# A new order of loads and steps in the first stage of a fused forgetting-attention and MLP kernel

## The chip, the cores and the metric

The kernel runs on one core of a Trainium2 chip. The metric is the device time of one execution in microseconds (us), the median over the runs of one comparison; lower is better. Profiles are of one execution each, with the engines TensorE (PE; PEld is its weight loads), VectorE (DVE), ScalarE (ACT), GpSimd (POOL) and SyncE (SP).

## The reference

Attention with a forget gate over 8 batches, 8 heads, 576 positions and 64 values per head, followed by an MLP over the 4608 tokens (512 to 2048 to 512) with a tanh GELU:

```python
scores = scale * np.matmul(q, k.transpose(0, 1, 3, 2))
cum = np.cumsum(np.log(np.clip(f, 0.0001, 1.0)), axis=-1)
scores = np.where(causal, -1e9, scores + cum[:, :, :, None] - cum[:, :, None, :])
attn = softmax(scores)                       # over keys
x = np.matmul(attn, v)                       # then (b, s) x (h, d): 4608 x 512
h = x @ w_in                                 # 512 x 2048
out = gelu_tanh(h) @ w_out                   # 2048 x 512
```

Inputs and output are float32.

## The kernel before

**Units of work.** The 64 pairs of batch and head are taken as 16 quads of four heads. Quad `i` belongs to batch `i // 2`. The MLP goes over 9 chunks of 512 tokens. For a quad, queries and keys are loaded as bf16 (`q_c`, `k_c`, two buffers each, by the parity of the quad), turned on VectorE (`qT`, `kT`), multiplied on TensorE in three score rounds (`ps_s`), put through the exponential on ScalarE into `pt`, masked on the diagonal, and multiplied with the values. The gate enters as a weight on each key: `vw` is v times this weight, and `w_bf` holds the weights that give the denominators.

**An order written out by hand.** There is no scheduler: the string `FRONT` (and `SECOND`, `STEADY`, `FLUSH`, `LAST` for later chunks) is a list of words, and `run` (L807) executes them one by one, which appends their instructions to the engines' queues. Every engine works through its own queue in that order and waits where an operand is not there yet or a buffer is still being read. What stands between two words on another engine's queue does not matter to an engine; what stands ahead on its own queue does. A word `X@Y` makes the load X wait also for Y (`after`, L176). The words that matter here, with the number of the quad or chunk as first argument:

- `LK.i`, `LQ.i`: load k or q of quad i, issued on GpSimd's queue (L208, 288 KB each). `LC.1.t`: tile t of v of batch 1, on GpSimd's queue too (L185, 256 KB; tile 4 is half). `LV.b.h`: half of v of batch b, on SP's queue, behind the stores of the output. `WI.n`, `WO.n`: pieces of w_in, and quarters of w_out (L201, 512 KB as bf16), on GpSimd's queue.
- `TK.i`, `TQ.i`: transposes of k and q on VectorE (L214).
- `S.i.r`: score round r of quad i on TensorE (L277) with its two exponentials on ScalarE (L285); `H.i.r.g` is half of one. Two buffers of PSUM serve the rounds.
- `M`: mask by a select on GpSimd (L291). `m`: mask by a product with a triangle on VectorE (L321).
- `VW.i`: `vw` of quad i on GpSimd (L231), `vw.i`: the same on VectorE. `CL.i`: copies 64 rows of `vw` on VectorE (L236).
- `D.i`: denominators: 24 matmuls (L347), then on VectorE den, rec and rb (L366 to L370). `V.i.x`, `v.i.x`: half of the attention output (L347), which VectorE multiplies by rb into `xT` (L379). The second group of matmuls of `V` reads the rows that `CL` copied. D and V share one PSUM buffer.
- `J`, `I.c.p`: first MLP product with GELU. `F.c.n`: the next n steps of the second MLP product of chunk c. For chunk 0 a step is one of 64 (four output tiles of 128 tokens, 16 steps of 128 hidden features each; L667). Quarter c of w_out serves steps 4c to 4c + 3 of each tile. When a tile is done, VectorE copies it (L672) and SP stores it; two PSUM buffers take turns. `F` uses a step as one matmul of the whole array, `f` as four matmuls of 32 columns.
- `U.k`, `UW.u.k`, `G`: sums of weight blocks and of GELU blocks on VectorE that save multiplications in later chunks. `X`: loads ScalarE's table for the exponential.

The loads on GpSimd's queue:

```python
def load_w_out(c):
    n = N_FT // 4
    return nc.gpsimd.dma_start(out=w_out_sb[:, n * c:n * (c + 1), :],
                        in_=w_out_hbm[:, n * c:n * (c + 1), :])
```

The functions that the words name, and the loop that reads them:

```python
def load_values(b, half):
    return load_v(b, 4 * half, 4)
...
"F": out_part,
"f": lambda c, n: out_part(c, n, 1),
```

Of the kernel before, what the change touches and what calls it, by code (L numbers as in the profile page):

```python
# [16 lines left out]
def kernel(  # L17
# [12 lines left out]
    B, H, S, D = q.shape  # L30
# [44 lines left out]
    FRONT = """  # L75
        Z TQ.0 LP.2 TR WI.1 TQ.1 S.0.0 B.1.384 CW WI.0 TK.1 S.0.2 LP.4 LP.3 B.1.512 vw.0.0 B.2.512 H.1.0.1 H.1.1.1 WI.3 M.0.0 W vw.1.0 WI.2 B.2.512
        WI.5 H.1.0.0 D.0.0 M.1.0.1 M.1.0.0 H.0.1.1 V.0.0.0 H.0.1.0 M.0.1 LQ.2 V.0.1.0 B.1.256 H.1.1.0 D.1.0 WI.4 H.0.3.0 WI.6 B.1.256 V.1.0.0 H.0.3.1
        WI.7 LK.2 V.1.1.0 m.0.3.2 H.1.3.0 j.0.0 vw.0.1 H.1.3.1 LC.1.4 m.0.3.4 D.0.1 M.1.3 S.1.2 M.1.1 VW.1.1 V.0.0.1 WO.0 V.0.1.1 LC.1.2 D.1.1
        WO.2@m.0.3.4 J.0.1 J.0.2 WO.1 LC.1.0@VW.1.1 WO.3@m.0.3.2 V.1.0.1 V.1.1.1 LC.1.1 GJ.0.0 LC.1.3 TK.2 J.1.1 LK.3 J.0.3 J.1.0 LQ.3 TQ.2 LQ.4 VW.3
        J.1.3 LK.4 J.1.2 F.0.4 X F.0.4 S.2.0 F.0.11 TK.3 S.2.2 F.0.6 LV.2.0 TQ.3 F.0.4 LK.5 S.2.1 F.0.2 F.0.7 TQ.4 m.2.1 S.3.0 vw.2 CL.2 M.2.2 f.0.7  # L80
        M.2.0 D.2 S.3.1 f.0.7 LQ.5 V.2.0 m.3.0 S.3.2 TK.4 LK.6@LQ.4 f.0.1 f.0.3 V.2.1 M.3.2 f.0.2 S.4.1 CL.3 m.3.1 LQ.6 f.0.5 TQ.5 H.4.2.1 D.3 H.4.0.1
        H.4.0.0 VW.4 V.3.1 v.3.0 f.0.1 H.4.2.0 U.0 m.4.1 LV.2.1@m.3.1 I.1.1 LQ.7@CL.3 I.1.4 TQ.6 I.1.6 m.4.2.3 I.1.0 m.4.2.2 I.1.5 CL.4 U.3 LV.3.0@LQ.7
        U.1 TK.6 I.1.2 M.4.0 U.2 G.0 TK.5 UW.2.1 I.1.3 I.1.7 G.1.1.2 F.1.16 X UW.2.2 S.5.0 UW.2.3 LQ.8 F.1.19 S.5.1 D.4 VW.5 M.5.0 f.1.13 S.5.2 V.4.0
        f.1.14 V.4.1 UW.2.4 m.5.2.3 m.5.2.2 CL.5 M.5.1 S.6.0 f.1.13 D.5 S.6.1 f.1.4 LK.7 V.5.1 f.1.3 f.1.10 vw.6 S.6.2 m.6.1 M.6.2.2 m.6.0 V.5.0
        LV.3.1@LK.6 f.1.5 CL.6 LK.8 m.6.2.3
    """

    SECOND = """
# [32 lines left out]
    def many(n, shape, dtype, name):  # L121
        return [singles.tile(shape, dtype, name=f"{name}{i}") for i in range(n)]
# [11 lines left out]
    vw = many(2, [128, NT + 1, 4, D], BF16, "vw")  # L134
# [724 lines left out]
```

## Time and profile before

| | before |
|---|---|
| time, median of 3 runs | 324.79 us (324.18 to 325.45) |
| profiled execution, its own time | 326.56 us |
| its span on the core | 324.3 us |
| TensorE busy | 310.0 us (96%) |
| VectorE busy | 241.7 us (75%) |
| ScalarE busy | 212.6 us (66%) |
| GpSimd busy | 107.0 us (33%) |
| granted TensorE clock | 1.0 of full speed |
| read from HBM, written | 36.85 MB, 9.44 MB |

A row of a timeline begins with its start and its duration in us from the start of the span, then the engine, the line of the kernel, the operation, what it writes and reads with shapes, how many instructions were merged, and in brackets the idle time of the engine ahead of it with what ended it. A row of waits gives the total, the number and the longest. A row of DMA issues gives the size and the time from issue to landing. The page's busy times are of the whole span. A matmul's end is modelled, so a wait on TensorE is better read from the starts of neighbouring rows.

### The profile page before, as it was taken

Reading aid. Unit: us, or ns where it says so; the run is one execution under the profiler, and the core shown is the slowest. Engines: PE = TensorE matmul, PEld = TensorE weight load, DVE = VectorE, ACT = ScalarE, POOL = GpSimd, SP = SyncE. Lnnn points to the kernel's source line nnn. Section 1 sums busy time; section 2 is a strip of 40 time slices with the busy share of each in tenths; the row PEclk is TensorE's granted clock in tenths of the full one; section 3 lists DMA queues with packets and bytes.
Section 4 is the critical chain, followed back from the end, with each engine's and each line's share of the span. In section 5 each row is a group of like instructions: output and inputs, shape, how many; then the busy total and the mean of one; then the engine's idle time right before and its main releaser. Section 6 shows DMA issues by size and latency. Waiting matters only on the chain.

```text
span 324.3 us, 11816 instructions
## 1 busy us (share of the span) xinstructions
PE 310.0 (96%) x5337; PEld 221.2 (68%) x5337; DVE 241.7 (75%) x374; ACT 212.6 (66%) x242; POOL 107.0 (33%) x145
## 2 busy tenths in 40 slices
PE   0799989999999999999999999999999999999996
PEld 0557844454677667776788877767776786788785
DVE  3664307998989978779876998599885866597574
ACT  4495667686766786678667876877587743846610
POOL 8868507253111405510752056305610150000000
PEclk9999999999999999999999999999999999999999
DMA  6999999577034951395119610981001011010202
GB/s 117 232 155 165 196 250 217 139 160 143 8 67 88 227 116 36 76 213 107 36 40 211 143 40 6 206 183 35 7 32 67 17 35 53 16 50 2 99 33 98
DMA packets 47490, 33.41 MB, mean 103 GB/s; under 512 B 29776, under 2 KB 42192, under 8 KB 47440
## 3 DMA queue, kind: packets, MB, share of 16 engines
q0 software_dynamic: 9632, 15.99, 28.4%
q1 hardware_dynamic: 37664, 16.60, 18.9%
q8 instruction: 41, 0.67, 0.8%
q14 instruction: 9, 0.07, 0.1%
q10 hardware_dynamic: 144, 0.07, 0.1%
HBM read 36.85 MB, written 9.44 MB: 143 GB/s over the span
## 4 chain that ended last, share of the span: by engine, by line
PE 82%; DMA 6%; POOL 4%; ACT 4%; DVE 2%; issue 1%; POOLq 0%; DVEq 0%
PE ps_w L600 30%; PE ps_h L395 19%; PE po L347 9%; PE ps_q L520 8%; PE ps_s L277 8%; DMA w_out_sb<-in_moe_w_out_dram 4%; PE ps_u L468 4%; PE pso L667 4%; DMA q_c<-in_q_dram 2%; ACT pt L285 2%; POOL pt L291 1%; POOL w_out_sb L201 1%; POOL v_nat L185 1%; POOL w_in_sb L197 1%; PE cum_ps L721 1%
## 5 line engine op out<-in xcount | busy, mean ns | idle before, releaser
L285 ACT ACTIVATE pt<-ps_s 128x1024 bf16<-128x1024 f32 (+2 forms) x100 | 93.9, 990 | 41.3 <-PE ps_s L277 37.1
L291 POOL TENSOR_SCALAR_AFFINE_SELECT pt<-pt 128x512 bf16<-128x512 bf16 (+3 forms) x65 | 40.8, 639 | 98.0 <-ACT pt L285 75.2
L395 PE MATMUL ps_h<-xT,w_in_sb 128*128 128x512 bf16 (+1 forms) x320 | 66.8, 358 | 0.3 <-ACT gT L403 0.2
L395 PEld LDWEIGHTS <-w_in_sb 128*128 128x128 bf16 x320 | 31.2, 98 | 26.7 <-issue 0.6
L600 PEld LDWEIGHTS <-gT 128*32 128x32 bf16 (+1 forms) x1216 | 44.2, 97 | 5.5 <-issue 2.2
L403 ACT ACTIVATE gT<-ps_h 128x1024 bf16<-128x1024 f32 x34 | 34.6, 1017 | 18.7 <-PE ps_h L395 18.4
L600 PE MATMUL ps_w<-w_out_sb,gT 128*32 128x256 bf16 (+1 forms) x1008 | 42.6, 273 | 0.0
L277 PE MATMUL ps_s<-qT,kT 32*128 32x64 bf16 (+5 forms) x896 | 36.3, 263 | 4.6 <-DVE qT L214 4.3
L600 PEld LDWEIGHTS <-gsum 128*32 128x32 bf16 (+1 forms) x948 | 35.5, 97 | 3.6 <-issue 1.3
L231 POOL TENSOR_TENSOR vw<-v_nat,wT 128x1280 bf16<-128x1280 f32 (+1 forms) x13 | 29.6, 2278 | 11.8 <-DMA v_nat<-in_v_dram 11.5
L536 DVE TENSOR_TENSOR usnap<-ps_q,usnap 128x1024 f32<-128x1024 f32 x15 | 17.9, 1222 | 18.6 <-PE ps_q L520 13.2
L277 PEld LDWEIGHTS <-kT 32*128 32x128 bf16 x896 | 16.5, 93 | 20.9 <-issue 11.5
L600 PE MATMUL ps_w<-usum,gsum 128*32 128x256 bf16 (+1 forms) x791 | 29.9, 273 | 0.0
L617 DVE COPY snap<-ps_w 128x512 f32<-128x512 f32 x32 | 21.8, 681 | 6.1 <-PE ps_w L600 6.0
L531 ACT ACTIVATE gT<-usnap 128x1024 bf16<-128x1024 f32 x15 | 15.8, 1054 | 12.1 <-DVE usnap L536 11.8
L379 DVE TENSOR_TENSOR xT<-po,rb 128x576 bf16<-128x576 f32 x26 | 19.5, 752 | 5.6 <-PE po L347 5.3
L347 PE MATMUL po<-pt,vw 128*32 128x64 bf16 (+4 forms) x624 | 22.4, 278 | 0.0
L214 DVE STREAM_TRANSPOSE qT<-q_c 128x576 f32<-128x576 f32 x16 | 19.8, 1247 | 2.7 <-DMA q_c<-in_q_dram 2.5
L214 DVE STREAM_TRANSPOSE kT<-k_c 128x576 f32<-128x576 f32 x16 | 19.5, 1248 | 3.1 <-DMA k_c<-in_k_dram 3.1
L347 PEld LDWEIGHTS <-vw 128*32 128x32 bf16 x672 | 14.8, 97 | 9.3 <-issue 2.8
L208 POOL DMA_DIRECT2D k_c<-in_k_dram x16 | 9.1, 569 | 33.7 <-DVE kT L214 17.4
L520 PEld LDWEIGHTS <-w_in_sb 128*128 128x128 bf16 x160 | 15.6, 98 | 2.5 <-issue 0.4
(134 smaller groups left out, 478.4 us busy)
## 6 DMA issues: line engine op xcount, KB each, us to landing
out_dram<-o_st SPq DMA_DIRECT2D x35, 256.0 KB, 2.3
k_c<-in_k_dram POOLq DMA_DIRECT2D x16, 288.0 KB, 5.2
q_c<-in_q_dram POOLq DMA_DIRECT2D x16, 288.0 KB, 6.2
v_nat<-in_v_dram SPq DMA_DIRECT2D x16, 256.0 KB, 5.3
v_nat<-in_v_dram SPq DMA_DIRECT2D x20, 128.0 KB, 4.9
v_nat<-in_v_dram POOLq DMA_DIRECT2D x8, 256.0 KB, 8.2
w_in_sb<-in_moe_w_in_dram POOLq DMA_DIRECT2D x8, 256.0 KB, 7.6
w_out_sb<-in_moe_w_out_dram POOLq DMA_DIRECT2D x4, 512.0 KB, 11.1
```

What stands on the lines that cost most here:

```text
L214: return nc.vector.transpose(out=dst.rearrange("p s c -> p (s c)").bitcast(FP32) .rearrange("p (t a) -> p a t", a=S // 32), in_=src.rearra ...
L231: return eng.tensor_mul(vw[i % 2][:, t0:t1], vb[:, t0:t1, h0:h0 + 4, :], wT[:, i, t0:t1, :].unsqueeze(3).to_broadcast([128, t1 - t0, 4, D]))
L277: nc.tensor.matmul(tiles[h // 2][:, h % 2, c0:c0 + nq], key_columns(i, key, h, c), qq[32 * h:32 * h + 32, q0:q0 + nq, c], start=(c == 0 an ...
L285: nc.scalar.activation(p[:, 2 * g:2 * g + 2, off:off + n], t[:, :, 0:n], AF.Exp, scale=scale)
L291: nc.gpsimd.affine_select(out=x, in_=x, compare_op=ALU.is_ge, fill=0.0, base=0, pattern=pattern, channel_multiplier=-1)
L347: nc.tensor.matmul(po[r0:r0 + w.shape[-1], 448 + q0:448 + q0 + nq], w, p[:, h, col:col + nq], start=(key in (0, "low")), stop=(key in ("lo ...
L379: nc.vector.tensor_mul(xT[:, 2 * u + x, r0 + s0:r0 + s1], po, rbs[i, part])
L395: nc.tensor.matmul(ph[:, j, n * cols:(n + 1) * cols], w_in_sb[:, dt, 128 * ft:128 * ft + 128], xT[:, dt, h0:h0 + cols], start=(dt == 0 and ...
L403: nc.scalar.activation(gelus(c, 2 * pr, 2), ph, AF.Gelu_apprx_tanh)
L520: nc.tensor.matmul(ps[:, k, HC * n:HC * n + HC], w[:, d, 128 * n:128 * n + 128], x[:, d, :], start=(first and n == 0 and d == 0), stop=(d ...
L600: nc.tensor.matmul(ps[c0:c0 + width, n, cols[0]:cols[1]], x[:, j, 128 * n + c0:128 * n + c0 + width], w[:, j, cols[0]:cols[1]], start=(fir ...
L617: copy(kept[name], ps)
```

## The change

Only the string `FRONT` changes, from the word behind `WI.7` on; no operation is added or taken away. What it does:

- The quarters of w_out are issued as 0, 1, 2, 3 one behind the other (before: 0, a v tile, 2, 1, a v tile, 3), then k and q of quad 3, then four tiles of v of batch 1, then `LQ.4` and `LK.4`.
- `VW.3` moves on GpSimd's queue from behind `LQ.4` to behind the masks `M.2.2` and `M.2.0`.
- On VectorE, `TK.3` and `TQ.3` move ahead of the first copy of an output tile, `TQ.4` behind `m.2.1` and `vw.2`, `CL.2` behind the denominators of quad 2.
- The 64 steps of chunk 0 are dealt out anew between the score rounds, most of them as `F`: before 4, 4, 11, 10, 9, 7, 7, 4, 2, 5, 1; after 9, 11, 10, 9, 8, 6, 2, 3, 5, 1.
- Later in the string `U.0`, `m.4.1`, `TK.4`, `VW.4`, `UW.2.1`, `UW.2.2`, `I.1.2`, `I.1.3`, `I.1.7` change places with neighbours, and `LV.3.1` waits for `LQ.7` instead of `LK.6`.

```diff
-        ... V.0.0.1 WO.0 V.0.1.1 LC.1.2 D.1.1
-        WO.2@m.0.3.4 J.0.1 J.0.2 WO.1 LC.1.0@VW.1.1 WO.3@m.0.3.2 V.1.0.1 V.1.1.1 LC.1.1 GJ.0.0 LC.1.3 TK.2 J.1.1 LK.3 J.0.3 J.1.0 LQ.3 TQ.2 LQ.4 VW.3
-        J.1.3 LK.4 J.1.2 F.0.4 X F.0.4 S.2.0 F.0.11 TK.3 S.2.2 F.0.6 LV.2.0 TQ.3 F.0.4 LK.5 S.2.1 F.0.2 F.0.7 TQ.4 m.2.1 S.3.0 vw.2 CL.2 M.2.2 f.0.7
-        M.2.0 D.2 S.3.1 f.0.7 LQ.5 V.2.0 m.3.0 S.3.2 TK.4 LK.6@LQ.4 f.0.1 f.0.3 V.2.1 M.3.2 f.0.2 S.4.1 CL.3 m.3.1 LQ.6 f.0.5 TQ.5 H.4.2.1 D.3 H.4.0.1
-        H.4.0.0 VW.4 V.3.1 v.3.0 f.0.1 H.4.2.0 U.0 m.4.1 LV.2.1@m.3.1 I.1.1 LQ.7@CL.3 I.1.4 TQ.6 I.1.6 m.4.2.3 I.1.0 m.4.2.2 I.1.5 CL.4 U.3 LV.3.0@LQ.7
-        U.1 TK.6 I.1.2 M.4.0 U.2 G.0 TK.5 UW.2.1 I.1.3 I.1.7 G.1.1.2 F.1.16 X UW.2.2 S.5.0 ...
+        ... V.0.0.1 WO.0 V.0.1.1 D.1.1 WO.1@m.0.3.4
+        J.0.1 J.0.2 WO.2 WO.3 LK.3 LQ.3 V.1.0.1 V.1.1.1 LC.1.2 LC.1.0@m.0.3.4 LC.1.3 GJ.0.0 LC.1.1 TK.2 J.1.1 J.0.3 TQ.2 J.1.0 J.1.3 LQ.4 LK.4 J.1.2
+        F.0.4 F.0.5 X TK.3 TQ.3 S.2.0 F.0.11 S.2.2 F.0.10 LV.2.0 LK.5 S.2.1 F.0.9 m.2.1 vw.2 S.3.0 TQ.4 F.0.8 M.2.2 M.2.0 D.2 VW.3 S.3.1 CL.2 F.0.6
+        LQ.5 V.2.0 m.3.0 TK.4 S.3.2 LK.6@LQ.4 f.0.2 M.3.2 V.2.1 F.0.1 f.0.2 S.4.1 CL.3 m.3.1 LQ.6 F.0.5 TQ.5 H.4.2.1 D.3 H.4.0.1 H.4.0.0 V.3.1 v.3.0
+        f.0.1 H.4.2.0 VW.4 m.4.1 U.0 LV.2.1@m.3.1 I.1.1 I.1.4 LQ.7@CL.3 UW.2.1 TQ.6 I.1.6 I.1.0 m.4.2.3 m.4.2.2 I.1.5 CL.4 U.3 LV.3.0@LQ.7 U.1 I.1.2
+        TK.6 M.4.0 U.2 I.1.3 I.1.7 G.0 TK.5 G.1.1.2 X UW.2.2 F.1.16 S.5.0 ...
```

## The prediction

> **What bounds the kernel now.** I read the page first, then TensorE's waits, then the timelines of TensorE, GpSimd and VectorE between 28 and 90 us, and last the DMA issues over short stretches, which give each load's time to landing.
>
> ```profile
> PE 310.0 (96%) x5337; PEld 221.2 (68%) x5337; DVE 241.7 (75%) x374; ACT 212.6 (66%) x242; POOL 107.0 (33%) x145
> ...
> PE 82%; DMA 6%; POOL 4%; ACT 4%; DVE 2%; issue 1%; POOLq 0%; DVEq 0%
> ```
>
> TensorE is busy 310.0 of 324.3 us; the first matmul group after the start-up begins at 9.86, and behind it almost nothing is idle. So a wait removed from TensorE shortens the kernel by its full length, a new one lengthens it by as much, and nothing later absorbs either. The chain's 6% of DMA is where to look. The waits of TensorE between 20 and 120 us have one row:
>
> ```profile
> PE pso L667 <- DMA w_out_sb<-in_moe_w_out_dram: 1.3, 2, 0.7
> ```
>
> ```profile
> 41.95 1.03 PE L667 MATMUL pso<-w_out_sb,gT 128*128 128x512 bf16 x4
> 43.58 1.02 PE L667 MATMUL pso<-w_out_sb,gT 128*128 128x512 bf16 x4 [0.60 <-DMA w_out_sb<-in_moe_w_out_dram]
> 44.53 0.70 PE L277 MATMUL ps_s<-qT,kT 32*128 32x64 bf16 x24
> 45.16 1.04 PE L667 MATMUL pso<-w_out_sb,gT 128*128 128x512 bf16 x4
> 46.86 1.67 PE L667 MATMUL pso<-w_out_sb,gT 128*128 128x512 bf16 x7 [0.66 <-DMA w_out_sb<-in_moe_w_out_dram]
> 48.47 0.63 PE L277 MATMUL ps_s<-qT,kT 32*128 32x320 bf16 x16
> 49.03 2.33 PE L667 MATMUL pso<-w_out_sb,gT 128*128 128x512 bf16 x10
> 51.30 0.64 PE L277 MATMUL ps_s<-qT,kT 32*128 32x64 bf16 x16
> 51.86 2.12 PE L667 MATMUL pso<-w_out_sb,gT 128*128 128x512 bf16 x9
> 53.91 0.74 PE L277 MATMUL ps_s<-qT,kT 32*128 32x64 bf16 x24
> ```
>
> A row's first number is its start. From start to start, ten F steps take 2.27 us and nine take 2.05: 0.22 each and 0.1 for the switch to scores. The four at 41.95 need 0.87 and hold 1.63 (43.58 - 41.95), so the first wait is really 0.76; the four at 45.16 hold 1.70, so the second is 0.83. The busy figure hides the tail of a matmul. Together the waits on w_out are **1.6 us**, all that the new order of loads can return.
>
> **The loads.** All these loads go through GpSimd's queue, and land in the order of issue. Landings before: quarter 0 of w_out 37.2, a v tile 38.0, quarter 2 41.0, quarter 1 43.5, a v tile 44.3, quarter 3 46.8, two v tiles 47.5 and 48.3, LK.3 49.6, LQ.3 51.0, LQ.4 52.5. The differences are prices: a quarter 2.5 to 3.1 us, a v tile 0.75, k or q of a quad 1.4. In the new order: quarter 0 at 37.2, quarters 1 and 2 at 40.3 and 42.8, quarter 3 at 46.8 less the two v tiles (1.5) = 45.3, LK.3 46.7, LQ.3 48.1, four v tiles to 51.1, LQ.4 52.5. The ninth load behind a given one waits for it (LK.3, issued at 37.48, for quarter 0), so the last two v tiles are issued behind the landing of quarters 0 and 1, at 37.4 and 40.4, ten us before their turn: free.
>
> F.4 F.5 now run from 41.95 to 44.0 and need quarter 2 at 43.7: no wait. S.2.0 to 44.6; F.11 asks for quarter 3 at 44.6 + 3 x 0.22 = 45.27: a wait of 0.1 (bounds 0 and, at 3.1 for each quarter, 1.3). Score rounds now follow at S.2.2 47.1, S.2.1 49.9, S.3.0 52.5 (before 48.5, 51.3, 53.9). ScalarE needs some 2.6 us from one round to the next in its buffers (51.30 to 53.91), and every new distance has that, F.9 exactly.
>
> **VectorE's order.** TK.3 and TQ.3 now stand ahead of the copy of output tile 0, so the copy waits for LQ.3: TQ.3 48.1 to 49.35, copy to 50.0. Tile 2 needs that buffer at the third step of F.9, 50.95: hidden by 0.9 us, beyond which each us that LQ.3 is late costs one.
>
> **F for f.** F replaces most f. A run of F that ends in an attention product pays the 0.1 us switch; column-wise f steps do not (28 matmuls, 7 steps, 54.58 to 56.10 = 1.52, nothing over). F.8 before D.2, F.6 before V.2.0 and F.1 between V.2.1 and f.2: 0.2 to 0.4 us; I take 0.35.
>
> **VW.3 moved behind M.2.0.** This decides the sign.
>
> ```profile
> 48.43 2.33 POOL L231 TENSOR_TENSOR vw<-v_nat,wT 128x1280 bf16<-128x1280 f32 x1 [6.34 <-DMA v_nat<-in_v_dram]
> 50.70 1.12 POOL L208 DMA_DIRECT2D k_c<-in_k_dram  x2
> 51.83 2.34 POOL L291 TENSOR_SCALAR_AFFINE_SELECT pt<-pt 128x512 bf16<-128x512 bf16 x4
> ```
>
> Before, VW.3 ran while VectorE did transposes. LK.4 and LK.5, no longer behind it, issue some 3 us sooner. The masks M.2.2 and M.2.0 start when the exponentials of S.2.2 end (48.47 to 51.12 before, so 47.1 + 2.65 = 49.8) and take 2.34, to 52.1; the v tiles are there at 51.1. VW.3 so holds GpSimd from **52.1 to 54.4**. On VectorE, m.2.1 becomes ready when S.2.1's exponentials end, 49.9 + 2.6 = 52.6, with vw.2 behind it. What such a meeting costs, the trace shows elsewhere:
>
> ```profile
> 78.31 2.33 POOL L231 TENSOR_TENSOR vw<-v_nat,wT 128x1280 bf16<-128x1280 f32 x1 [5.15 <-DMA v_nat<-in_v_dram]
> 79.02 2.16 DVE L578 TENSOR_TENSOR gsum<-gT 128x1024 bf16<-128x1024 bf16 x1 [1.24 <-ACT gT L403]
> ...
> 81.83 0.68 DVE L580 TENSOR_TENSOR gsum<-gsum,gT 128x1024 bf16<-128x1024 bf16 x1
> ```
>
> The same VW form made a VectorE operation of 0.68 us last 2.16, ending 0.54 behind it; transposes beside VW keep their 1.25. m.2.1 and vw.2 are operations on two SBUF operands, like the one slowed. The Trainium skill ("SBUF — State Buffer", section "SBUF: two separate sides") says that a VectorE operation with two SBUF inputs and a GpSimd operation that reads SBUF share a port pair under an exclusive lock, whole instruction by whole instruction, not a split of bandwidth. By this rule m.2.1 waits out VW.3; by a split, it would stretch by 0.4 and the whole change would come out near 1 us faster. The 2.16 us row is on the side of the lock.
>
> So m.2.1 ends at 54.8 instead of 53.0, vw.2 (1.47) at 56.2, TQ.4 (1.25) at 57.45, and the den, rec, rb of D.2 (57.01 to 58.91 before: 1.9) run only now, to 59.4; CL.2, which the change puts behind them, ends at 59.65. TensorE does D.2 at 55.0 (m.2.1 just there), S.3.1 55.8, F.6 56.4, V.2.0 at 57.8, whose second group of matmuls reads CL.2's rows at 58.05: a new wait of **1.6 us**. Without the lock TQ.4 ends at 55.7, den starts when D.2 ends (55.95), CL.2 ends at 58.1: wait 0.05. If m.2.1 wins the race for the port instead (0.5 us of margin), VW.3 still gets in ahead of vw.2 and the wait is 2.1. Queued behind CL.2 on VectorE are the copy of tile 2 and the xT product of V.2.0, which end in time for V.2.1. VW.3 itself is read by V.3.1, ten us later. Bounds 0 and 2.1; I take 1.6, from the nearest row.
>
> **The rest in one go.** U.0, m.4.1, TK.4, VW.4 and UW.2.1 change places among neighbours; UW.2.1 (0.41) goes into the 1.24 us that VectorE idles before the sum at 79.02, and if that cover were gone it would cost 0.41 of a sum that TensorE needs only two products later. I.1.3 and I.1.7 keep their place on TensorE. The gate of LV.3.1 names another load that has landed long before. Nothing.
>
> **Sum.** -1.6 (waits on w_out) + 0.1 (quarter 3) + 0.35 (switches) + 1.65 (CL.2) = +0.5 us. The profiled execution took 326.56 around a span of 324.3; it becomes 327.1 and 324.8. The median of the unprofiled runs, 324.79, lies 0.5% under the profiled one; the sum is carried onto it: **325.3**.
>
> **Rivals.** First, no collision, or one that V.2.0 does not see: the masks or the v tiles come so that vw.2 has begun before VW.3 is ready (after 53.0). Then the sum is -1.6 + 0.1 + 0.35 + 0.05 = -1.1, 323.7. For it: only half a us decides the order. Against it: a late VW.3 queues ahead of vw.2 rather than behind it. Second, slower: the four v tiles, now behind four quarters and LK.3, LQ.3, land late. m.2.1 is then through first, VW.3 and vw.2 both wait for the tiles, and V.2.0 waits for their landing + 2.3 (VW.3) + 1.5 (vw.2) + 1.25 (TQ.4) + 2.2 (den to CL.2), less 58.05. It decides from a landing at 52.5 on, 1.4 us late, and each further us costs one: at 53.6 that is a wait of 2.8 and a sum of +1.65, at 54.5 +2.6 (327.4). For it: quarters at 3.1 each put everything 1.3 later, and the first store and LV.2.0 on SP's queue start at 50. Against it: LQ.3 and LQ.4 kept 1.4 each beside such loads at 49 to 52. The Trainium skill ("DMA: Bandwidth & Descriptors", section "Queues, rings and completion order") has each DMA engine take turns between queues, which would halve the pace of the last v tile only and bring 51.1 to about 51.7, an estimate; no run here shows that case alone. Third, the order of the quarters does not help since quarter 3 lands where it did: the wait is 1.5 instead of 0.1 and the time 326.7; its landing at 46.8 held two v tiles that are gone, so little speaks for it.
>
> **How the numbers follow.** What a measurement of this kernel can tell from no change is about 0.5%, 1.6 us. Forecast 0.60 (its own range 324.4 to 326.2), no collision 0.20 (323.2 to 324.3), late tiles 0.12, quarter 3 unmoved 0.04, something that gains more than all the waits on w_out 0.04. Faster by over 0.5% would need 323.2: 0.04. Slower, over 326.4: the late tiles, and half of the third rival with the forecast's upper tail, 0.16. Within: 0.80. The range 323.4 to 326.8 leaves out most of the late tiles and the lower tail of the first rival.
>
> **What would show it.** TensorE's row on w_out gone or under 0.3 us; VW.3 on GpSimd at 52, m.2.1 on VectorE lasting some 2 us instead of 0.41; CL.2 at 59 to 60; and a TensorE wait of 1 to 2 us at V.2.0, the only new one. Wrong: m.2.1 at 0.4 us beside VW.3, V.2.0 without a wait, or TensorE waiting at F.9 for the copy of tile 0.

## The result and the profile after

The change makes the kernel slower: 329.15 us, median of 6 runs (328.10 to 330.49), against 324.92 us of the kernel before in the same comparison (6 runs, 323.55 to 325.85). The ratio is 1.0137, 95% interval [1.0102, 1.0171]: 4.2 us, where 0.5 were forecast. The profiled execution took 329.89 us around a span of 328.1 (before: 326.56 and 324.3).

The whole difference lies in one stage. From the first step of F to the first matmul of I.1.1 the kernel before takes 27.19 us (41.95 to 69.14), the kernel after 31.84 (41.22 to 73.06): 4.65 more. From there to the end both take the same, 255.1 us. (The start-up ended 0.73 sooner in this execution, which is why the spans differ by 3.8 only.)

The page of the kernel after, its busy line and the chain that ended last:

```profile
PE 310.9 (95%) x5255; PEld 221.2 (67%) x5274; DVE 247.1 (75%) x374; ACT 212.8 (65%) x242; POOL 107.7 (33%) x145
...
PE 79%; DMA 6%; DVE 5%; ACT 4%; POOL 3%; issue 2%; DVEq 0%; POOLq 0%
```

VectorE has the same 374 instructions as before and 5.4 us more busy time, and its share of the chain went from 2% to 5%. TensorE's waits between 20 and 120 us (total, times, longest):

```profile
PE po L347 <- DVE pt L321: 2.5, 1, 2.5
PE po L347 <- DVE vw L236: 1.0, 1, 1.0
...
PE pso L667 <- DMA w_out_sb<-in_moe_w_out_dram: 0.2, 1, 0.2
```

The waits on w_out are gone but for 0.2, the wait on CL.2 (L236) is there as forecast, and there is one that no step of the forecast had: 2.5 us on a mask product (L321). VectorE's timeline between 52 and 68 us shows whose fault it is:

```profile
52.23 2.29 DVE L321 TENSOR_TENSOR pt<-pt,causal 128x512 bf16<-128x512 bf16 x1 [0.74 <-ACT pt L285]
...
58.82 0.22 DVE L236 COPY vw<-vw 64x256 bf16<-64x256 bf16 x1
...
62.68 4.40 DVE L236 COPY vw<-vw 64x256 bf16<-64x256 bf16 x1
67.11 0.42 DVE L321 TENSOR_TENSOR pt<-pt,causal 128x512 bf16<-128x512 bf16 x1
```

The rows are m.2.1, CL.2, CL.3 and m.3.1. CL.3 is the same copy as CL.2, and lasts twenty times as long. GpSimd's timeline has the work that stands beside it:

```profile
51.91 2.33 POOL L231 TENSOR_TENSOR vw<-v_nat,wT 128x1280 bf16<-128x1280 f32 x1
...
62.36 0.53 POOL L208 DMA_DIRECT2D k_c<-in_k_dram  x1 [7.58 <-DVE kT L214]
62.90 1.24 POOL L291 TENSOR_SCALAR_AFFINE_SELECT pt<-pt 128x512 bf16<-128x512 bf16 x2
64.08 0.55 POOL L208 DMA_DIRECT2D q_c<-in_q_dram  x1
64.65 2.34 POOL L231 TENSOR_TENSOR vw<-v_nat,wT 128x1280 bf16<-128x1280 f32 x1
```

CL.3 asks 0.32 us into the issue of LK.6 and ends 0.09 behind VW.4 (64.65 + 2.34 = 66.99; 62.68 + 4.40 = 67.08). It was shut out through LK.6, the two selects of M.3.2, LQ.6 and VW.4, while none of these lasted longer than alone. m.3.1 comes behind it, and D.3 on TensorE needs m.3.1. In the kernel before the same two operations, from its VectorE timeline, met the same row of GpSimd's, LK.6, M.3.2, LQ.6, VW.4 (its first two entries are shown below them, from GpSimd's timeline):

```profile
62.90 0.22 DVE L236 COPY vw<-vw 64x256 bf16<-64x256 bf16 x1
63.15 0.78 DVE L321 TENSOR_TENSOR pt<-pt,causal 128x512 bf16<-128x512 bf16 x1
```

```profile
62.44 0.53 POOL L208 DMA_DIRECT2D k_c<-in_k_dram  x1 [7.78 <-ACT pt L285]
63.02 1.40 POOL L291 TENSOR_SCALAR_AFFINE_SELECT pt<-pt 128x512 bf16<-128x512 bf16 x2
```

There CL.3 ran at once, inside LK.6's issue, and m.3.1 got in between the two selects.

Then the clock. Short windows of the kernel after; the columns are the window's length, the busy time of PE, PEld, DVE, ACT and POOL with the instructions of each, the granted TensorE clock, the DMA share and GB/s:

```profile
67.00:67.50 0.50, 0.00 (x0) 0.00 (x0) 0.47 (x3) 0.00 (x0) 0.00 (x0) 1.00 0.39 76
...
68.50:69.00 0.50, 0.50 (x22) 0.18 (x10) 0.50 (x2) 0.08 (x1) 0.00 (x0) 0.80 0.11 33
69.00:69.50 0.50, 0.35 (x8) 0.24 (x8) 0.47 (x2) 0.50 (x1) 0.49 (x1) 0.50 0.00 0
...
71.00:72.00 1.00, 1.00 (x25) 0.66 (x20) 0.68 (x1) 0.00 (x0) 0.94 (x2) 0.50 1.06 196
72.00:72.50 0.50, 0.50 (x14) 0.18 (x8) 0.25 (x1) 0.00 (x0) 0.07 (x1) 0.79 0.13 19
72.50:73.00 0.50, 0.50 (x8) 0.23 (x9) 0.50 (x2) 0.00 (x0) 0.00 (x0) 1.00 0.03 5
```

TensorE stood still from about 65.07 to 67.59. From 68.8 to 72.2 its granted clock is one half (the windows at 0.80 and 0.79 are mixtures), with work in every window. So the 4.65 us are: 0.64 up to D.3 (22.78 us behind the first F step before, 23.42 after; the forecast sum was 0.5), some 2.7 of standstill, and 1.3 of half clock behind it.

### The profile page after: what moved, and what is told of

Read it like the earlier page. It is cut to its first block, busy times and chain, and to the rows that moved or that the text cites. A ratio compares the mean times of both kernels' runs of the same rounds, so it can differ in the third digit from the quotient of the medians.

```text
span 328.1 us, 11669 instructions
## 1 busy us (share of the span) xinstructions
PE 310.9 (95%) x5255; PEld 221.2 (67%) x5274; DVE 247.1 (75%) x374; ACT 212.8 (65%) x242; POOL 107.7 (33%) x145
## 4 chain that ended last, share of the span: by engine, by line
PE 79%; DMA 6%; DVE 5%; ACT 4%; POOL 3%; issue 2%; DVEq 0%; POOLq 0%
PE ps_w L600 30%; PE ps_h L395 18%; PE po L347 9%; PE ps_q L520 8%; PE ps_s L277 7%; DMA w_out_sb<-in_moe_w_out_dram 4%; PE ps_u L468 4%; ACT pt L285 2%; DMA q_c<-in_q_dram 2%; DVE vw L236 1%; PE pso L667 1%; DVE qT L214 1%; POOL pt L291 1%; PE cum_ps L721 1%; POOL w_out_sb L201 1%
## 5 line engine op out<-in xcount | busy, mean ns | idle before, releaser
L395 PE MATMUL ps_h<-xT,w_in_sb 128*128 128x512 bf16 (+1 forms) x307 | 65.6, 357 | 1.1 <-ACT gT L403 0.2
L231 POOL TENSOR_TENSOR vw<-v_nat,wT 128x1280 bf16<-128x1280 f32 (+1 forms) x13 | 30.3, 2331 | 1.9 <-DMA v_nat<-in_v_dram 1.6
L347 PE MATMUL po<-pt,vw 128*32 128x64 bf16 (+4 forms) x624 | 23.2, 284 | 1.3 <-DVE vw L236 1.0
```

What stands on the lines that cost most here:

```text
L231: return eng.tensor_mul(vw[i % 2][:, t0:t1], vb[:, t0:t1, h0:h0 + 4, :], wT[:, i, t0:t1, :].unsqueeze(3).to_broadcast([128, t1 - t0, 4, D]))
L347: nc.tensor.matmul(po[r0:r0 + w.shape[-1], 448 + q0:448 + q0 + nq], w, p[:, h, col:col + nq], start=(key in (0, "low")), stop=(key in ("lo ...
L395: nc.tensor.matmul(ph[:, j, n * cols:(n + 1) * cols], w_in_sb[:, dt, 128 * ft:128 * ft + 128], xT[:, dt, h0:h0 + cols], start=(dt == 0 and ...
```

## The experiments

All are timed against the kernel before, at 324.66 to 325.35 us in the various comparisons. "The stage" is the stretch from the first F step to I.1.1, 27.19 us before and 31.84 after. An edit is given by the words of FRONT that it changes.

**1. CL.3 out of the way.** In the kernel after, CL.3 directly behind CL.2.

```diff
-S.3.1 CL.2 F.0.6 ... S.4.1 CL.3 m.3.1
+S.3.1 CL.2 CL.3 F.0.6 ... S.4.1 m.3.1
```

> The changed kernel with one word moved: CL.3 (the copy of 64 rows of vw of quad 3, 0.22 us on VectorE before, 4.40 us after the change) stands directly behind CL.2, where GpSimd computes nothing, instead of behind S.4.1, where GpSimd has the masks M.3.2 and VW.4. Theory A (the copy lost the SBUF port to GpSimd and held up m.3.1, for which D.3 waited 2.5 us on TensorE; the clock of TensorE then fell and cost another 1.3 us): CL.3 takes 0.2 us, m.3.1 ends before D.3 wants it, the granted clock stays at 1.0, and the kernel is some 4 us faster than the changed kernel: about 325.1, that is +0.1 to +0.8 us on the kernel before. Rival B (m.3.1 or D.3 was late for something else, such as the exponentials or the loads of k and q, and the copy only shows the wait): D.3 still waits over 2 us and the time stays at 328 to 330.

329.06 us, ratio 1.0120 [1.0087, 1.0153]. CL.3 took its 0.2 us at 57.2, and m.3.1, now first in the line, became the one shut out:

```profile
60.83 4.70 DVE L321 TENSOR_TENSOR pt<-pt,causal 128x512 bf16<-128x512 bf16 x1
```

GpSimd's row began with LK.6 at 60.62 and ended with VW.4 at 65.24. The forecast of about 325.1 failed, and it isn't the copy as such: of these two operations, whichever comes then is hit. In this profiled execution the last v tile landed later, VW.3 began only at 52.56, and m.2.1 and vw.2 went ahead of it: my first rival, in one execution, and V.2.0 did not wait on CL.2. The clock stayed at 1.00 in the stage although TensorE waited 2.25 us for m.3.1; this execution took 327.01, the other five 328.3 to 330.1. The mean clock of the whole execution was 0.998 in this one and one more, and 0.994 to 0.995 in the other four, near the 0.990 to 0.995 of the kernel after, which points to the fall in those four.

**2. CL.3 on ScalarE.** The same copy, at the same place, by another engine (and `LQ.7` no longer waits for it).

```diff
-    nc.vector.tensor_copy(vw[i % 2][64:128, LOW], vw[i % 2][0:64, 0])
+    nc.scalar.copy(vw[i % 2][64:128, LOW], vw[i % 2][0:64, 0])
```

> The changed kernel with CL.3 at its place in the order, but done by ScalarE instead of VectorE, so the same bytes move at the same point and VectorE does not queue behind them. Theory A (an SBUF port that VectorE and GpSimd share): ScalarE's copy takes under 0.5 us beside the same GpSimd work, D.3 waits less than 0.3 us, time 325 to 326. Rival C (the rows of vw themselves are held, by VW.3 still writing or by V.1 still reading): ScalarE's copy waits as long as VectorE's did, V.3.1 waits in place of D.3, time 327 to 329.

329.76 us, ratio 1.0143 [1.0104, 1.0183]. ScalarE's copy took 0.40 us and was not held up; m.3.1 took 4.71 (62.41 to 67.12) against LK.6 to VW.4 (62.20 to 66.82). So the rows of `vw` are not what is held (rival C), and ScalarE is not shut out where VectorE is. The time did not fall because m.3.1 was hit in the copy's place.

**3. TensorE kept busy.** Twelve matmuls on idle data ahead of D.3, which add nothing to the output.

```diff
-TQ.5 H.4.2.1 D.3 H.4.0.1
+TQ.5 H.4.2.1 K.12 D.3 H.4.0.1
```

> The changed kernel with 12 matmuls of 512 columns on idle data (2.6 us at full clock) put ahead of D.3 on TensorE, so that TensorE computes where it now stands still from 64.9 to 67.6 us; the output is the reference's. The wait of D.3 itself stays. If the fall of the granted clock to 0.5 to 0.7 between 68 and 72 us comes from that standstill, the clock stays at 1.0, V.3.1 takes 0.8 us instead of 1.3, and the kernel is 1.0 to 1.4 us faster than the changed one: about 327.9. If the fall has another cause (the load of the stage, or chance), the clock falls all the same and the time is 329.2 or a little more.

328.91 us, ratio 1.0126 [1.0097, 1.0155]. CL.3 still lasts 4.40, but the clock does not fall. The windows of this kernel that answer to 68 to 72 of the kernel after, same columns:

```profile
68.00:70.00 2.00, 1.73 (x52) 0.97 (x48) 1.97 (x3) 0.63 (x1) 0.55 (x1) 1.00 0.03 6
70.00:72.00 2.00, 2.00 (x60) 1.27 (x52) 1.86 (x4) 1.31 (x2) 0.59 (x3) 1.00 0.65 94
```

The mean clock is 0.999 to 1.000 in all six executions, so the fall of the clock follows from the standstill. The stage is 30.36 us, 1.48 shorter. Of that 0.39 lies ahead of D.2, which comes 13.09 us behind the first F step here and 13.48 in the kernel after; the other 1.1 comes behind it, near the 1.3 that I had put the half clock at. The whole time does not show this: it is only 0.2 lower than that of the kernel after, where 1.0 to 1.4 were expected. The profile has two new stalls of some 0.9 us without a releaser, at 33 us and at 99 us; what they are, and whether they eat the gain in the other executions too, stays open.

**4. CL.2 back behind vw.2**, in the kernel after: the forecast's own term taken away.

```diff
-m.2.1 vw.2 S.3.0 ... S.3.1 CL.2 F.0.6
+m.2.1 vw.2 CL.2 S.3.0 ... S.3.1 F.0.6
```

> The changed kernel with CL.2 moved back directly behind vw.2, ahead of TQ.4 and of the den, rec and rb of D.2, as in the kernel before. Theory A2: V.2.0's waits of 0.2 and 1.0 us on TensorE shrink to the 0.2 for den. What happens then at CL.3 hangs on who asks for the port first, CL.3 or GpSimd's queue of LK.6, M.3.2, LQ.6 and VW.4: if CL.3 is again late, 328.0 to 328.5; if it gets in ahead of them as in the kernel before, some 324.0 to 324.5. Rival: V.2.0 waits for vw.2 or den rather than for CL.2, then nothing changes.

329.6 us, ratio 1.0157 [1.0116, 1.0198], no better than the kernel after. In the profile V.2.0 and V.2.1 wait 0.9 us together (0.56 for den, 0.37 for xT) instead of 1.2, CL.3 lasts 4.40 and D.3 waits 2.6. The stage is 31.14 us, 0.7 shorter, of which the median shows nothing.

**5. LK.6 moved behind VW.4** on GpSimd, all else as after.

```diff
-S.3.2 LK.6@LQ.4 f.0.2 M.3.2 ... H.4.2.0 VW.4 m.4.1
+S.3.2 f.0.2 M.3.2 ... H.4.2.0 VW.4 LK.6@LQ.4 m.4.1
```

> The changed kernel with one load moved on GpSimd's queue: LK.6 is issued behind VW.4 instead of ahead of M.3.2; every other queue is as in the changed kernel. In all four kernels with the slow operation (4.4 to 4.7 us, CL.3 or, with CL.3 out of the way, m.3.1), it asked for the port 0.2 to 0.3 us into the issue of LK.6 and got it when VW.4 ended, the last of LK.6, M.3.2, LQ.6, VW.4, which run without a pause. Theory A3 (a VectorE operation that asks during the issue of a GpSimd load stays shut out until GpSimd's queue pauses): with LK.6 out of the way CL.3 asks while GpSimd waits for the exponentials, takes 0.22, m.3.1 takes 0.4 to 0.8, D.3 does not wait, the clock stays at 1.0, the stage from the first F step to I.1.1 takes 27.8 us instead of 31.8, and the time is 325 to 326. Rival D (it is shut out by the run of masks and VW.4 itself, whatever is issued ahead): CL.3 or m.3.1 still takes over 3 us and the time is 328 to 330.

325.82 us (12 runs), ratio 1.0017 [0.9994, 1.0040]. CL.3 now asks while M.3.2's first select runs (GpSimd's timeline, then VectorE's):

```profile
60.85 1.22 POOL L291 TENSOR_SCALAR_AFFINE_SELECT pt<-pt 128x512 bf16<-128x512 bf16 x2 [7.59 <-ACT pt L285]
```

```profile
61.16 0.40 DVE L236 COPY vw<-vw 64x256 bf16<-64x256 bf16 x1
61.59 0.76 DVE L321 TENSOR_TENSOR pt<-pt,causal 128x512 bf16<-128x512 bf16 x1
```

It gets in between the selects, m.3.1 behind them, D.3 does not wait, the clock stays, and the stage is 27.42. This one move returns nearly all of the loss. By the ratio it costs 0.55 us on the kernel before, which is what the prediction's sum gave, though the interval reaches from no change to 1.3 us.

**6. VW.4 moved behind LQ.7**, LK.6 where it was.

```diff
-H.4.2.0 VW.4 m.4.1 ... LQ.7@CL.3 UW.2.1
+H.4.2.0 m.4.1 ... LQ.7@CL.3 VW.4 UW.2.1
```

> The changed kernel with VW.4 moved behind LQ.7 on GpSimd's queue, and LK.6 left where it is. VW.4 is first read 30 us later. Both A3 and D say that CL.3 is shut out until GpSimd's queue pauses, which it now does behind LQ.6, 2.3 us sooner: CL.3 takes about 2.1 us instead of 4.4, D.3 waits 0.2 to 0.5 us instead of 2.7, the clock stays at 1.0, and the time is 325.3 to 326.5. If the end of the wait has nothing to do with VW.4 (it ends when a load lands, say, or after a fixed time), CL.3 keeps its 4.4 us and the time stays at 328 to 330.

325.69 us, ratio 1.0019 [0.9998, 1.0040], stage 27.52. CL.3 asks 0.32 into LK.6's issue as in the kernel after, and lasts 1.54 (62.12 to 63.66): to the end of M.3.2 (63.58), not of LQ.6 (64.07). So the end of the row can be cut off, and the issue of LQ.6 alone did not hold CL.3 out.

**7. The loads alone**: the kernel before with the new order of loads, VW.3 still behind LQ.4.

```diff
-VW.1.1 V.0.0.1 WO.0 V.0.1.1 LC.1.2 D.1.1 WO.2@m.0.3.4 J.0.1 J.0.2 WO.1 LC.1.0@VW.1.1 WO.3@m.0.3.2 ...
+VW.1.1 V.0.0.1 WO.0 V.0.1.1 D.1.1 WO.1@m.0.3.4 J.0.1 J.0.2 WO.2 WO.3 LK.3 LQ.3 ... LC.1.2 LC.1.0@m.0.3.4 LC.1.3 ... LC.1.1 ...
```

> The kernel before with the first part of the change alone: the quarters of w_out in order, k and q of quad 3 behind them, then the four v tiles; VW.3 stays behind LQ.4 and all other orders stay. The waits on w_out (1.6 us) should go down to 0.0 to 0.3. What it costs: VW.3 now waits on GpSimd for the last v tile at some 51.4, runs to 53.7, and with it LK.4, LK.5 and the masks M.2.2 and M.2.0 of quad 2 are late; they end near 57.2, where D.2 wants them at 54.6: a new wait of 1.5 to 2.7 us at D.2. Sum -0.2 to +1.3 us: 324.5 to 326, so the loads need VW.3 moved to be worth anything. Rival: D.2 does not wait on the masks, then -1.4 us, 323.4.

330.85 us, ratio 1.0183 [1.0149, 1.0218]: slower than the kernel before, by its median slower than the kernel after too (the intervals overlap), and far from what I expected. VW.3 waits for the last v tile until 51.49 and holds up LK.4, LK.5 and the masks of quad 2 behind it, which vw.2 stretches besides (from GpSimd's timeline):

```profile
51.49 2.33 POOL L231 TENSOR_TENSOR vw<-v_nat,wT 128x1280 bf16<-128x1280 f32 x1 [8.24 <-DMA v_nat<-in_v_dram]
...
54.90 3.60 POOL L291 TENSOR_SCALAR_AFFINE_SELECT pt<-pt 128x512 bf16<-128x512 bf16 x4
```

D.2 waits 4.1 us for these masks, and the clock falls to one half behind that too. The loads can't have their new order without VW.3 moving. But CL.3 lasts 0.22 here: the new order of loads is not what shuts it out.

**8. Experiments 4 and 5 together, and VW.3 held until CL.2 is done**, in the kernel after.

```diff
-m.2.1 vw.2 S.3.0 ... D.2 VW.3 S.3.1 CL.2 F.0.6 LQ.5 V.2.0 ... S.3.2 LK.6@LQ.4 ... VW.4 m.4.1
+m.2.1 vw.2 CL.2 S.3.0 ... D.2 LQ.5@CL.2 VW.3 S.3.1 F.0.6 V.2.0 ... S.3.2 ... VW.4 LK.6@LQ.4 m.4.1
```

> A version that takes the gain and leaves the collisions out: the changed kernel with CL.2 directly behind vw.2, LK.6 behind VW.4, and LQ.5, now ahead of VW.3 on GpSimd's queue, waiting for CL.2, so that VW.3 starts when m.2.1, vw.2 and CL.2 are through. By the sum: -1.6 (waits on w_out) + 0.1 + 0.35 (switches of TensorE) + 0 at V.2.0 and D.3 = -1.2 us on the kernel before: 323.6, range 323.0 to 324.6. If a new collision takes the place of the old ones (VW.3 now beside m.3.0, or CL.3 against M.3.2), 325 or more.

324.13 us (12 runs) against 324.98, ratio 0.9976 [0.9956, 0.9997]: clearly faster than the kernel after, and faster than the kernel before by an interval that only just leaves out no change. VW.3 runs at 54.59, beside transposes; m.2.1 takes 0.43, CL.3 0.39. TensorE's only waits between 40 and 75 us are

```profile
PE pso L667 <- issue: 0.6, 3, 0.3
PE pso L667 <- DMA w_out_sb<-in_moe_w_out_dram: 0.3, 1, 0.3
```

(the row "issue" stands for three steps of F that are missing from the records). The stage is 26.43, 0.76 shorter than in the profile of the kernel before. That profile has longer waits than others of its kind, though: in experiments 9, 10, 13 and 15 below, whose loads up to this stage are those of the kernel before and which have no collision, the same stage takes 26.63, 26.85, 26.17 and 26.33 us, with waits on w_out of 0.7, 0.9, 0.4 and 0.6 us where the kernel before has 1.3. So the gain is to be read from the medians: 0.8 us (0.1 to 1.4 by the interval), of 1.2 expected, is what the whole change was worth once its two collisions were gone.

**9 to 11. Is it the moment of asking?** In the kernel before CL.3 asks 0.46 us into LK.6's issue, in the kernel after 0.32. Three kernels shift that: a memset of 0.15 us ahead of LK.6 in the kernel before, V.2.1 two steps sooner in the kernel before, V.2.1 two steps later in the kernel after.

```diff
-TK.4 LK.6@LQ.4 f.0.1 f.0.3 V.2.1 M.3.2 f.0.2
+TK.4 P.6 LK.6@LQ.4 f.0.1 f.0.3 V.2.1 M.3.2 f.0.2
+P: nc.gpsimd.memset(k_c[i % 2][:, 0, :], 0.0)
```

> The kernel before, unchanged but for one memset of 128x64 bf16 on GpSimd ahead of LK.6, into the buffer that LK.6 fills, so that it runs only when TK.4 has ended and pushes LK.6's issue back by some 0.15 to 0.3 us (a memset of 64x64 bf16 took 0.14). It is on an engine that has been idle for 7.8 us there, and no data are computed differently. Theory A (it is the moment at which VectorE asks, within GpSimd's issue of LK.6, that decides): the issue moves from 62.44 to some 62.65-62.75, CL.3 asks at 62.90, now 0.15 to 0.25 into the issue instead of 0.46, is shut out until VW.4 ends and lasts some 4.4 to 4.7 us (if it should still slip in ahead, m.3.1 behind it is the victim); D.3 waits some 2.3 to 2.7, and the time goes from 324.9 to 327.5-329.5. Rival (the collision needs something else that the change brought, such as the order or the loads, or before's margin is not what keeps it clear): CL.3 0.22, m.3.1 0.8, time 324.5 to 325.5.

```diff
-f.0.1 f.0.3 V.2.1 M.3.2 f.0.2
+f.0.1 f.0.1 V.2.1 M.3.2 f.0.4
```

> The kernel before with two steps of f (0.22 us each) moved from ahead of V.2.1 to behind it; nothing else. V.2.1 then starts 0.44 us sooner (60.76 instead of 61.20), so that its xT product follows TK.4 on VectorE without a gap, 1.10 us after TK.4's start instead of 1.22, as in the kernel after. LK.6 keeps 1.55 us behind TK.4's start. Theory A (narrowed: a VectorE operation on two SBUF sides, or a copy within SBUF, that asks 0.2 to 0.35 us into GpSimd's issue of LK.6 is shut out until VW.4 ends; one that asks at 0.46 is not): CL.3 asks 0.32 into the issue instead of 0.46 and lasts 4.4 us instead of 0.22, D.3 waits some 2.5 us, the clock falls, and the time goes from 325 to 328-329.5. Rival (the collision needs what the change did earlier, such as VW.3 behind the masks): CL.3 0.22, time 324.7 to 325.5.

```diff
-f.0.2 M.3.2 V.2.1 F.0.1 f.0.2
+f.0.4 M.3.2 V.2.1 f.0.1
```

> The kernel after with two steps of F moved from behind V.2.1 to ahead of it; nothing else. V.2.1 starts 0.44 us later (61.12 instead of 60.68), its xT product at about 62.03 instead of 61.91, CL.3 asks at about 62.81, 0.45 into LK.6's issue (62.36) as before the change, instead of 0.32. Theory A: CL.3 0.22, m.3.1 0.8, no wait at D.3, clock 1.0, and all of the forecast's other terms stay (V.2.0 still waits 1.2 on CL.2): time 325 to 325.8 instead of 329.1. Rival: CL.3 still 4 us or more, time 328.5 to 329.5.

Measured: 325.30 us (ratio 1.0000 [0.9983, 1.0018]; CL.3 asks at 0.13 and lasts 0.22), 325.25 (1.0017 [1.0002, 1.0033]; asks at 0.32, lasts 0.24), 329.92 (1.0168 [1.0150, 1.0186]; asks at 0.46, lasts 4.27). The theory fell: the very moment that was fatal after the change is harmless before it, and the other way round.

**12 and 13. Is it the wait of M.3.2?** The instructions in the traces show that M.3.2's first select also waits for GpSimd's own earlier work in the kernel before, and for ScalarE alone in the kernel after. One kernel puts such a wait in, the other takes it out; every engine keeps its order.

```diff
-f.0.2 M.3.2 V.2.1 F.0.1
+f.0.2 M.3.2@VW.3 V.2.1 F.0.1
```

> The kernel after with one wait more and every instruction of every engine in the same order: the first select of M.3.2 also waits for VW.3, an instruction of its own engine that ended 8 us earlier, so that the wait itself costs nothing. Theory W: in the kernel before this select waits for ScalarE and for an earlier GpSimd instruction, and GpSimd's queue passes it on only when LK.6's issue has ended (the queue's next semaphore event 62.97, the issue's end 62.97, the select 0.05 behind it); in the kernel after it waits for ScalarE alone, is passed on behind LK.6 while that is still issuing (next event 62.84, select 0.01 behind the issue), and the port is taken for the row LK.6, M.3.2, LQ.6, VW.4. With the second wait put back, CL.3 lasts 0.22-0.25 us, m.3.1 0.4-0.9, D.3 waits nothing, the clock stays, and the time is 325.0-326.0 (as with LK.6 moved: 325.8). Rival (theory A, the moment of asking, or the rest of the order): CL.3 4.4 us, 328.5-329.8.

```diff
-f.0.7 LQ.5 V.2.0 m.3.0
+f.0.7 LQ.5@M.2.0 V.2.0 m.3.0
```

> The kernel before with one wait moved and every instruction in the same order: LQ.5's load, directly behind M.2.0 on GpSimd, waits for M.2.0's last select, so that the first select of M.3.2 no longer needs its own wait on an earlier GpSimd instruction and waits for ScalarE alone, as in the kernel after. LQ.5 runs behind M.2.0 anyway (0.05 us at most). Theory W: the select is passed on while LK.6 still issues, and the VectorE operation that asks in that time, CL.3, is shut out until VW.4 ends: 4.0-4.7 us, D.3 waits some 2.5, the clock falls, and the kernel before becomes as slow as the kernel after, 327.5-329.5. Rival: CL.3 0.22 and 324.5-325.5, nothing changed.

329.35 us (1.0141 [1.0114, 1.0167], CL.3 4.40) and 324.73 (0.9995 [0.9974, 1.0015], CL.3 0.22). Neither flips.

**14 and 15. Is it GpSimd's last computation ahead of LK.6?** A memset there in the kernel after, a small product (1.57 us) there in the kernel before, both behind LQ.5 and in idle time.

```diff
-LQ.5 V.2.0 m.3.0 TK.4
+LQ.5 P V.2.0 m.3.0 TK.4
+P: nc.gpsimd.memset(scrap, 0.0)
```

> The kernel after with one memset of 128x64 bf16 into a buffer that nothing reads, on GpSimd directly behind LQ.5, in the 7.6 us in which GpSimd idles before LK.6. Nothing else. Theory L (GpSimd's last computation ahead of LK.6's issue decides): in every kernel with the long operation it was VW.3, a product, and the select began 0.01 us behind the issue; in every kernel with a short one it was a select or a memset, and the select began 0.05 to 0.06 behind the issue. With the memset in between, CL.3 lasts 0.22 to 0.3 us, m.3.1 0.4 to 0.9, the select begins 0.05 behind the issue, D.3 waits nothing, the clock stays: 325.0 to 326.0 us. Rival (the last computation is a bystander too): CL.3 4.4, 328.5 to 329.8.

```diff
-f.0.7 LQ.5 V.2.0
+f.0.7 LQ.5 P V.2.0
+P: nc.gpsimd.tensor_mul(scrap, scrap, scrap)
```

> The kernel before with one product of 128x64 bf16 by itself, in a buffer that nothing else uses, on GpSimd directly behind LQ.5 (and a memset of it at the start); it makes a product the last computation ahead of LK.6, instead of the selects of M.2.0. Theory L: the select of M.3.2 begins 0.01 us behind LK.6's issue, CL.3, which asks in that issue, is shut out until VW.4 ends and lasts 4.0 to 4.7 us, D.3 waits some 2.5, the clock falls, and the time is 327.5 to 329.5. Rival: CL.3 0.22, 324.5 to 325.5.

329.76 us (1.0160 [1.0143, 1.0177], CL.3 4.40) and 325.06 (1.0008 [0.9991, 1.0024], CL.3 0.36). Neither flips.

**16 and 17. Which part of the change is it?** VW.3 moved behind M.2.0 in the kernel before, with its old loads and old orders; and VW.3 put back ahead of LK.4 in the kernel after.

```diff
-LQ.4 VW.3 J.1.3 LK.4 ... M.2.0 D.2 S.3.1
+LQ.4 J.1.3 LK.4 ... M.2.0 D.2 VW.3 S.3.1
```

> The kernel before with VW.3 alone moved behind M.2.0 on GpSimd; its loads, and the order on every other engine, as before. Theory P (what shuts CL.3 out depends on VW.3 standing behind the masks): CL.3 or m.3.1 lasts 4 us or more and D.3 waits, 327.5 to 330 us. Rival (it is something else in the new order: TensorE's, VectorE's or ScalarE's): CL.3 0.2 to 0.4, m.3.1 0.4 to 0.8; besides, VW.3 meets vw.2 and CL.2 at 53 to 57, which may cost V.2.0 up to 1 us: 324.5 to 326.

```diff
-LQ.4 LK.4 ... D.2 VW.3 S.3.1
+LQ.4 VW.3 LK.4 ... D.2 S.3.1
```

> The kernel after with VW.3 put back ahead of LK.4 on GpSimd; loads and all other orders as after. VW.3 then waits for the last v tile (51.4) and the masks run behind it and behind LK.4 and LK.5, to 57 or 58.5: D.2 waits some 3 to 4 us and the clock falls, as in the kernel with the loads alone (330.85), so that the whole time says little (328 to 331). The question is CL.3 alone: theory P says 0.2 to 0.4 us, the rival 4 us or more.

Both flip. VW.3 alone, on VectorE's timeline:

```profile
52.87 2.31 DVE L321 TENSOR_TENSOR pt<-pt,causal 128x512 bf16<-128x512 bf16 x1
...
62.12 4.40 DVE L236 COPY vw<-vw 64x256 bf16<-64x256 bf16 x1
```

330.29 us, ratio 1.0171 [1.0138, 1.0204], with the waits on w_out (1.4 us) still there. VW.3 put back, on VectorE's timeline:

```profile
66.88 0.23 DVE L236 COPY vw<-vw 64x256 bf16<-64x256 bf16 x1
```

Its whole time, 330.54 (1.0174 [1.0142, 1.0206]), comes from D.2's wait on the masks (3.7 us), as in experiment 7. So it is the place of VW.3 on GpSimd's queue that decides whether CL.3 is shut out, ten microseconds after VW.3 starts; the new loads and the new orders of TensorE, ScalarE and VectorE are not needed for it. (With its place VW.3 also shifts LK.4, LK.5 and the masks, which come ahead of it or behind it.) Nor is it the earlier meeting of VW.3 with VectorE. In experiment 17 VW.3 meets vw.2, which is shut out for more than 2 us, and CL.3 still runs at once:

```profile
52.90 3.62 DVE L231 TENSOR_TENSOR vw<-v_nat,wT 128x1280 bf16<-128x1280 f32 x1
```

In experiment 1 m.2.1 took 0.43 us and vw.2 1.49, neither held up, and m.3.1 was shut out all the same. How a product that ended 8 us earlier decides this is open: the moment of asking, M.3.2's wait and the kind of GpSimd's last computation are excluded by experiments 9 to 15.

The half clock was also longer in the profile of experiment 16. It was 0.50 in every window from 66.5 to 73.0 us, 6.8 us in all and twice the 3.4 of the kernel after; it began while D.3 still waited (until 67.03), and the stage took 33.15 us.

## Why the prediction was wrong, point by point

- *Waits on w_out, -1.6 and +0.1*: right in mechanism, and too large. Quarter 3 landed at 44.9 (forecast 45.3), k and q of quad 3 at 46.3 and 47.85, the last v tile at 51.4 (forecast 51.1). But F began 0.73 sooner, so the wait that is left is more than 0.1: 0.2 by the profile's row, and 0.4 by starts, as the 1.6 was measured (three steps need 0.66, and 43.89 to 44.95 is 1.06). And the 1.6 was read from one execution: in five other profiles of kernels with the old order of loads (experiments 9, 10, 13, 15 and 16) the same rows give 0.4 to 1.4 us, where the kernel before gave 1.3.
- *The copy of tile 0 behind TQ.3*: right; it ran at 48.98, and TensorE did not wait for it.
- *VW.3 moved behind M.2.0, the meeting with m.2.1*: right in mechanism. VW.3 ran 51.91 to 54.24 (forecast 52.1 to 54.4), m.2.1 lasted 2.29, CL.2 ran at 58.82, and V.2.0 waited 1.2 us (0.2 on den, 0.97 on CL.2) instead of 1.65 (by starts, 1.4). Experiment 1 showed the first rival, no collision, in one execution; experiment 14 showed the other case that the prediction names, m.2.1 first and VW.3 ahead of vw.2, which lasted 3.62.
- *Up to D.3 the sum holds*: +0.64 measured, +0.5 forecast. By starts it is -1.2 for the loads, +1.4 at V.2.0 and the rest, 0.4, for the switches (forecast -1.5, +1.65 and +0.35). That +0.64 comes so near is partly luck of the two executions: the kernel before has D.3 at 22.78 us in this profile, its kin of experiments 9, 10, 13 and 15 at 21.77 to 22.45, and the kernel after's 23.42 is 23.02 in experiments 5 and 6. Pairs of these give +0.6 to +1.7. Experiment 5, which takes away only what comes behind, measured 325.82 against my 325.3.
- **The step that failed** is the end of "VW.3 moved behind M.2.0. This decides the sign": "Queued behind CL.2 on VectorE are the copy of tile 2 and the xT product of V.2.0, which end in time for V.2.1. VW.3 itself is read by V.3.1, ten us later." I closed the account of the move there. The next meeting of VectorE with GpSimd, CL.3 and m.3.1 against the row LK.6, M.3.2, LQ.6, VW.4, stood in the trace of before, went well there, and I took it to go well again. Experiment 16 shows that the move of VW.3 alone turns it into 4.40 us, and so into D.3's wait of 2.5 us.
- *"nothing later absorbs either"*: true behind I.1.1, but the forecast gave a wait its own length only. The standstill at D.3 also halved the clock for 3.4 us, 1.3 us more by the stage (experiment 3: 1.1 of it comes back there when TensorE is kept busy).
- *The rivals*: none named this meeting. The late tiles did not come in the profile of the kernel after; the third rival was wrong (quarter 3 came early).

The Trainium skill ("SBUF — State Buffer", section "SBUF: two separate sides") has VectorE and GpSimd take the shared port pair one whole instruction at a time. m.2.1 agrees: 2.29 us, ending 0.28 behind VW.3. CL.3 does not: it waited through three computations of GpSimd and two issues of loads (4.40 us), and was let in after the first select in experiment 5 (0.40 us). The measurement decides: the price of such a meeting can be a whole row of GpSimd's work.

The Trainium skill ("TensorE: Matmul & The Clock Gate", section "What's actually happening") names two states of the clock, full and half, and a window of about 3.4 us that runs on by itself. The trace agrees: 1.00, then 0.50 for 3.4 us, then 1.00. The Trainium skill's rule in the section "Why this matters for your kernels" of the same text, to avoid gaps above about 3 us, was not enough: 2.5 us brought the fall here, and 2.3 us in experiment 2.

## What to carry to other kernels

When a GpSimd operation is moved, don't close its account at its neighbours: go through every later place where a VectorE operation with two SBUF operands, or a copy within SBUF, meets a run of GpSimd work, and price it with the whole run as the bad end of the range, even where it went well before. Moving one load's issue from the head of such a run to its end (experiment 5) was worth 3.3 us here. And price a standstill of TensorE of 2.3 to 2.5 us or more with the half clock that can follow it: 3.4 us of it here, 6.8 us in experiment 16, none in the profile of experiment 1 (2.25 us).

## What the runs showed of the hardware that I had not expected

- A VectorE operation that normally takes 0.2 to 0.4 us can last 4.3 to 4.7 us beside a run of GpSimd work that begins with the issue of a load (kernel after, experiments 1 to 4, 11, 12, 14, 16); when the run has no VW.4, 1.54 (experiment 6).
- Whether that happens was decided by the place of an operation that had ended 8 us earlier (experiments 16 and 17), not by the moment within 0.3 us (9 to 11).
- ScalarE's copy beside the same run took 0.40 us (experiment 2).
- In the kernel after the granted clock fell only 1.2 us after TensorE had resumed work (68.8 against 67.6), and stayed at one half for 3.4 us of work; in experiment 16 it fell during the standstill and stayed for 6.8 us.
